# Loading and decoding weight pieces on two separate schedules, and one chunk's P in another place

## The chip, the cores and the metric

The kernel runs on one core of a Trainium2 chip. The metric is the device time of one execution in microseconds (us). The engines are TensorE (PE in the rows, PEld for its weight loads), VectorE (DVE), ScalarE (ACT), GpSimd (POOL) and SyncE (SP, which here only issues transfers).

## The reference

Three parts stand behind one another. The first is a recurrence over 768 steps, for 4 batches and 8 heads, with a state of 40 x 40:

```python
for t in range(S):
    y[:, :, t] = einsum('bhd,bhde->bhe', r_t, state)
    Sa = einsum('bhde,bhe->bhd', state, a_t)
    state = state * w_t[:, :, None, :] - einsum('bhd,bhe->bhde', Sa, b_t)
    state = state + einsum('bhd,bhe->bhde', v_t, k_t)
x = y.transpose(0, 2, 1, 3).reshape(3072, 320)
x = ((x @ w1) * (x @ w2)) @ w3 @ w_out          # w1, w2: 320x1024, w3: 1024x1024, w_out: 1024x320
out = square(maximum(x @ w_in, 0)) @ w_out2     # w_in: 320x2048, w_out2: 2048x320
```

## The kernel before

**The recurrence** runs in 24 chunks of 32 steps. For each chunk the inputs are prepared some chunks ahead: `prep` loads an image of the inputs (`im<-img`, `iw<-img`), forms running products of w with scans on VectorE (`suf`, `wi`) and multiplies them in (`im<-im,wi`, `im<-im,suf`, GpSimd); `pq` makes the chunk's P and Q on TensorE (`Pn`, `qt`, lines 597 to 605); `kb` transposes and stores k and b (`kn`, then `KB_d<-kn`, lines 614 to 619). What is prepared goes through DRAM: `AW_d`, `Q_d` and `KB_d` are written and read again. For four chunks together `solve(k)` (lines 645 to 668) inverts triangular matrices on VectorE: transposes into PT, 31 pairs of a product `tmp` and a subtraction `T`, transposes out to `tt`. The first solve (chunks 0 to 3) is followed by a small `corner` step on TensorE (`x`, `tt`, lines 690 to 701). Each chunk then goes through x0 (`X`), sa (`SA`), sat (`vs`), l (`YI`), z (`YR`) and ys (`RX`, the state for the next chunk, and `yst`, the result, stored as `X_d<-yst`).

**The weights** arrive as 64-bit floats, that is two 32-bit words for each value. A piece (512 KB) is loaded into a `raw` or `early` tile and decoded by four instructions: on ScalarE `wst<-raw` (the high words, line 325) and in place `raw<-raw` (the low words, line 326), on VectorE two that put them together (lines 328 and 330). The 16 pieces of w3 are then folded with w_out on TensorE: 64 products `pw`, `step(f, k)`, four for each piece, into `wph` and `wpl`. The 8 whole pieces and 2 pieces of remaining rows (two loads each) of w1 and w2 are split into a high and a low part: a cast on ScalarE (`w1h<-wst`, line 340), a subtraction on GpSimd (`w1l<-wst,w1h`, line 341). For every two chunks `a_tile` computes 256 columns of (x @ w1) * (x @ w2) and their product with the folded weight (`ab`, line 370; `px`, line 428), as work that fills TensorE between the chunk's steps. When the recurrence is through, the last stage does the third part of the reference (`ph`, line 370; `po`, line 997), which takes the rest of the time.

**What sets the order.** TensorE's order is written by hand: two tables, `OPENING` and `BETWEEN`, say which `prep`, `pq`, `kb`, `corner` and `solve` stand between the steps of the first chunks, and after each step `Fill.pull(gap)` puts in items of a queue (folds, then A tiles). On the other engines a scheduler orders the instructions by priority; the chunk's steps run at a high one, items of the kind "decode" in the queue at none. An item of length 0 is issued when the items ahead of it have been pulled. Each engine does its instructions in its order: one that waits holds what stands behind it. All loads and stores named here are issued by SyncE.

Of the kernel before, what the change touches and what calls it, by code (L numbers as in the profile page):

```python
# [18 lines left out]
DM = 320  # L19
# [29 lines left out]
FOLD_NS = 535  # L49
SPLIT_AT = (8, 13)  # L50
W3_FIRST = 5
FOLD_STAGED = 8
SPLIT_STAGED = 8
# [190 lines left out]
def body(tc, img, rv, rd, vn, vp, raw, w1, w2, w3t, wo, win, wo2, ident, maskt, out, dbg=None):  # L244
# [4 lines left out]
    with (  # L249
# [12 lines left out]
        with right, tc.manual_schedule(engines={mybir.EngineType.PE}):  # L262
# [4 lines left out]
            fill = Fill(tc)  # L267
# [13 lines left out]
            early = True  # L281
# [10 lines left out]
            count = {"fold": 0, "split": 0}  # L292
            bufs = {"raw": WB[0], "wst": WB[1], "split": WB[2]}

            def fetch(pl, K, N, parts, dst=None, tag="fold"):

                place = None
                if early:
                    count[tag] += 1
                    if tag == "split" and count[tag] <= SPLIT_STAGED:  # L300
                        place = staged(ma, ("gh", "gl"), 1024)
                    elif tag == "fold" and not w12 and count[tag] <= FOLD_STAGED:
                        place = staged(wa, ("w1h", "w1l", "w2h"), 640)
                tag = "split" if early and tag == "split" else "wst"
                if dst is not None:
                    o = dst
                else:
                    o = pl.tile([128, K, N], F32, name="wst", tag=tag, bufs=bufs[tag])
                if not is64:
                    for p, f, src in parts:  # L310
                        sp.dma_start(out=o[p, f], in_=src)
                    return o
                if place is not None:
                    rt = place[:, 0:2 * K * N]
                else:
                    rt = pl.tile([128, 2 * K * N], U32, name="raw", tag="raw", bufs=bufs["raw"])
                rv_ = rt.rearrange("p (k n) -> p k n", k=K)
                for p, f, src in parts:
                    sp.dma_start(out=rv_[p, f], in_=src)
                w2_ = rt.rearrange("p (k n j) -> p k n j", k=K, j=2)  # L320
                hi, lo = w2_[:, :, :, 1], w2_[:, :, :, 0]
                ou = o.bitcast(U32)
# [11 lines left out]
            def split_w(pl, src, h, l, j, k):  # L334

                n = 512 if early else 256

                t = fetch(pl, 1, n, [(slice(0, 128), 0, wcols(src, n * j, n)[128 * k:128 * k + 128])], tag="split")
# [4 lines left out]
            def split_r(pl, two):  # L343

                n = 512 if early else 256


                t = fetch(pl, 1, n, [(slice(64 * i, 64 * i + 64), 0, wcols(src, c, n)[256:320])
                                       for i, (src, c, _) in enumerate(two)], tag="split")
                for i, (_, c, r) in enumerate(two):  # L350
                    p, q = slice(64 * i, 64 * i + 64), slice(64 - 64 * i, 128 - 64 * i)
                    f = slice(c, c + n)
                    act.copy(out=r[p, f], in_=t[p, 0])
                    pool.tensor_tensor(out=r[q, f], in0=t[p, 0], in1=r[p, f], op=ALU.subtract)
# [18 lines left out]
            def a_tile(n):  # L373
# [63 lines left out]
                fill.push((0, load, "load"), (0, split, "load"), before="x")  # L437
# [7 lines left out]
            def fold(solved):  # L445
# [9 lines left out]

                def step(f, k):
# [10 lines left out]
                def split12(j):  # L467
# [3 lines left out]
                    for k in range(2):  # L471
                        for src, t in zip((w1, w2), w12):
                            split_w(wf, src, *t[0:2], j, k)
                    split_r(wf, [(src, 512 * j, t[2]) for src, t in zip((w1, w2), w12)])

                hold.append(solved)
                for i in range(8):
                    fetch(wf, 1, DM, [(slice(0, 128), 0, wcols(wo)[128 * i:128 * i + 128, :])], dst=wo_sb[:, i:i + 1])
                for i in range(W3_FIRST):
                    load_w3(i)  # L480
                hold.clear()
                items = []
                for f in range(8):
                    for k in range(8):
                        items.append((FOLD_NS, lambda f=f, k=k: step(f, k), "w"))
                        i = 2 * f + k // 4
                        if k % 4 == 3:
                            if i + W3_FIRST < 16:
                                items.append((0, lambda i=i + W3_FIRST: load_w3(i), "decode"))
                            for j in range(2):  # L490
                                if SPLIT_AT[j] == i:
                                    items.append((0, lambda j=j: split12(j), "decode"))
# [447 lines left out]
            def wu(pl, k):  # L940
                t = fetch(pl, 1, DM, [(slice(0, 128), 0, wcols(wo2)[128 * k:128 * k + 128, :])])
                act.copy(out=wuh[:, k], in_=t[:, 0])
                pool.tensor_tensor(out=wul[:, k], in0=t[:, 0], in1=wuh[:, k], op=ALU.subtract)
# [3 lines left out]
            early = False  # L947
            bufs.update(raw=BB[0], wst=BB[1])
            for j in range(8):
                for k in range(2):  # L950
                    split_w(wst, win, wih, wil, j, k)
                if j < 4:
                    split_r(wst, [(win, 256 * j + 1024 * i, wir) for i in range(2)])
                for k in (2 * j, 2 * j + 1):
                    wu(wst, k)
                if j == 0:
                    b_split(wb, 0, 1)
                fill.pull(BP)
# [178 lines left out]
```

## Time and profile before

| what | us |
| --- | --- |
| median of 3 runs | 1073.65 |
| lowest and highest of them | 1069.87, 1074.45 |
| the profiled execution | 1071.28 |
| its span, from first to last instruction | 1069.5 |
| PE busy | 918.1 (86%) |
| DVE busy | 712.5 (67%) |
| ACT busy | 443.8 (41%) |
| POOL busy | 233.2 (22%) |

All busy times are of the span. They are averages over parts that differ: the recurrence with the A tiles takes until 714 us, the last stage the rest.

### The profile page before, as it was taken

How to read it: one execution, taken by the hardware profiler on the slowest of the kernel's cores; microseconds unless marked ns; L12 is line 12 of the kernel's file. 1: busy time of each engine (PE TensorE's matmuls, PEld its weight loads, DVE VectorE, ACT ScalarE, POOL GpSimd, SP SyncE). 2: the span in 40 equal slices, each digit the busy share in tenths (PEclk: the TensorE clock that was granted, in tenths of full speed). 3: DMA queues.
4: the chain of work that ended last, by engine and by line, in shares of the span. 5: the costliest groups of instructions: out<-in, count | busy, mean ns of one | idle time of the engine just before them, and what ended most of it. 6: DMA issues, size and time to landing. Idle time of an engine off the chain costs nothing.

```text
span 1069.5 us, 29225 instructions
## 1 busy us (share of the span) xinstructions
PE 918.1 (86%) x12240; PEld 822.5 (77%) x12240; DVE 712.5 (67%) x1399; ACT 443.8 (41%) x942; POOL 233.2 (22%) x304
## 2 busy tenths in 40 slices
PE   1327777688989889979899999889999999999997
PEld 1315545588888878979798889868989898898896
DVE  6864879957975997798489444887456554444432
ACT  2424556343434423424343434775334333333332
POOL 0271224433343343533200000652000000000000
PEclk9999888899999999989899999989999999999999
DMA  8976785666666567766644542665122121000001
GB/s 212 307 235 177 209 247 158 171 168 170 163 154 173 148 151 182 170 170 149 164 118 110 136 96 60 171 188 111 30 62 53 59 48 25 2 25 1 18 8 28
DMA packets 208922, 134.45 MB, mean 126 GB/s; under 512 B 143741, under 2 KB 184062, under 8 KB 208368
## 3 DMA queue, kind: packets, MB, share of 16 engines
q1 hardware_dynamic: 201424, 110.61, 40.6%
q0 software_dynamic: 7072, 21.57, 7.1%
q8 instruction: 99, 1.62, 0.7%
q10 hardware_dynamic: 288, 0.33, 0.2%
q14 instruction: 39, 0.32, 0.1%
HBM read 99.27 MB, written 33.19 MB: 124 GB/s over the span
## 4 chain that ended last, share of the span: by engine, by line
PE 48%; DVE 26%; DMA 12%; issue 5%; ACT 4%; POOL 3%; SPq 2%; ACTq 0%; DVEq 0%; POOLq 0%
PE ph L370 16%; PE po L997 15%; PE ab L370 6%; DMA im<-img 5%; DVE tmp L656 4%; PE px L428 4%; DVE T L659 4%; PE pat L800 2%; DVE RX L808 2%; DVE yst L812 2%; DVE gl L408 2%; DVE g L402 1%; DVE wst L328 1%; DVE YI L777 1%; POOL im L584 1%
## 5 line engine op out<-in xcount | busy, mean ns | idle before, releaser
L997 PE MATMUL po<-wul,rh 128*128 128x320 f32 x384 | 118.3, 308 | 0.0
L997 PE MATMUL po<-wuh,rh 128*128 128x320 f32 x384 | 118.0, 308 | 0.0
L997 PE MATMUL po<-wuh,rl 128*128 128x320 f32 x384 | 116.9, 308 | 0.0
L407 ACT CAST gh<-g 128x256 fp32r<-128x256 f32 x96 | 39.0, 406 | 99.8 <-DVE g L402 86.5
L370 PE MATMUL ph<-xh,wih 128*128 128x512 f32 x192 | 76.0, 396 | 0.7 <-issue 0.7
L428 PE MATMUL px<-wph,gh 128*128 128x320 f32 x192 | 68.1, 355 | 9.3 <-DVE x L433 4.8
L370 PE MATMUL ph<-xh,wil 128*128 128x512 f32 x192 | 75.7, 394 | 0.0
L370 PE MATMUL ph<-xl,wih 128*128 128x512 f32 x192 | 75.6, 394 | 0.0
L997 PEld LDWEIGHTS po<-wul,rh 128*128 128x128 f32 x384 | 72.0, 188 | 4.2
L997 PEld LDWEIGHTS po<-wuh,rh 128*128 128x128 f32 x384 | 72.0, 188 | 3.8
L997 PEld LDWEIGHTS po<-wuh,rl 128*128 128x128 f32 x384 | 71.6, 188 | 0.6 <-DVE rl L984 0.6
L800 PE MATMUL pat<-YI,YR 128*40 128x72 f32 (+1 forms) x1536 | 58.8, 240 | 13.7 <-DVE qt L602 8.1
L800 PEld LDWEIGHTS pat<-YI,YR 128*40 128x40 f32 x1536 | 54.5, 127 | 19.2 <-DVE qt L602 9.7
L408 DVE TENSOR_TENSOR gl<-g,gh 128x256 fp32r<-128x256 f32 x96 | 48.2, 503 | 30.0 <-ACT gh L407 29.6
L401 ACT COPY a_sb<-ab 128x256 f32<-128x256 f32 x96 | 35.6, 371 | 76.4 <-PE ab L370 75.9
L656 DVE TENSOR_TENSOR tmp<-PT,T 128x31 f32<-128x31 f32 (+20 forms) x170 | 64.9, 382 | 3.4
L659 DVE TENSOR_TENSOR T<-T,tmp 128x31 f32<-128x31 f32 (+20 forms) x170 | 64.5, 380 | 3.0
L428 PE MATMUL px<-wph,gl 128*128 128x320 f32 x192 | 63.2, 329 | 3.4 <-DVE gl L408 3.4
L584 POOL TENSOR_TENSOR im<-im,suf 104x256 f32<-104x256 f32 x80 | 64.4, 836 | 0.0
L428 PE MATMUL px<-wpl,gh 128*128 128x320 f32 x192 | 62.4, 325 | 0.0
L370 PE MATMUL ph<-xq,wir 128*128 128x512 f32 x192 | 60.1, 394 | 0.0
L370 PE MATMUL ab<-xh,w1h 128*128 128x256 f32 x192 | 57.9, 302 | 2.5 <-ACT xh L357 2.2
(539 smaller groups left out, 2444.3 us busy)
## 6 DMA issues: line engine op xcount, KB each, us to landing
raw<-w3t SPq DMA_DIRECT2D x16, 512.0 KB
YR<-KB_d SPq DMA_DIRECT2D x48, 160.0 KB
im<-img POOLq DMA_DIRECT2D x28, 240.0 KB, 4.5
wt<-AW_d SPq DMA_DIRECT2D x24, 214.5 KB
raw<-wo SPq DMA_DIRECT2D x16, 320.0 KB
RX<-vp SPq DMA_DIRECT2D x24, 208.0 KB
vs<-rv SPq DMA_DIRECT2D x24, 208.0 KB
KB_d<-kn POOLq DMA_DIRECT2D x14, 320.0 KB, 5.3
```

Source lines behind the costliest of these rows:

```text
L370: mm(out=ps, lhsT=seq[i][0], rhs=seq[i][1], start=(i == 0), stop=(i == 7))
L401: act.copy(out=a_sb, in_=ps[:, 0])
L407: act.copy(out=t["gh"][:, ff], in_=g)
L408: dve.tensor_tensor(out=t["gl"][:, ff], in0=g, in1=t["gh"][:, ff], op=ALU.subtract)
L428: mm(out=ps, lhsT=a_, rhs=b_, start=(k == 0 and i == 0), stop=(k == 7 and i == 2))
L584: eng.tensor_tensor(out=kb[:, g, :, :, j], in0=kb[:, g, :, :, j], in1=sg, op=ALU.mult)
L656: dve.tensor_tensor(out=tv, in0=Pv[:, :, s, s + 1:n].unsqueeze(3).to_broadcast(sh), in1=Tv[:, :, s, 0:s + 1].unsqueeze(2).to_broadcast(sh) ...
L659: return dve.tensor_tensor(out=o, in0=o, in1=tv, op=ALU.subtract).ins
L800: mm(out=ps[64 * y:64 * y + D, b, 72 * z:72 * z + n], lhsT=YR[:, u], rhs=YI[:, u, 0:n], start=True, stop=True, tile_position=(0, 64 * y))
L808: dve.tensor_tensor(out=o, in0=v[r, :, :, C:72], in1=decay.unsqueeze(3).to_broadcast([D, 2, HZ, D]), op=ALU.mult)
L812: dve.tensor_tensor(out=yst[r, :, 2 * g:2 * g + 2].rearrange("p z b t -> p b z t"), in0=v[r, :, :, 0:C], in1=wt[c][r, 2 * g:2 * g + 2, :, ...
L997: mm(out=po[j][g], lhsT=a_, rhs=b_, start=(ff == 0 and i == 0), stop=(ff == 15 and i == 2))
```

## The change

A function `fetch` that loaded and decoded a piece becomes two, `fetch` (load) and `decode`. The pieces of w3 are now put in the queue apart: behind the four folds of piece i stands the decode of piece i + 3 (`AHEAD`) and the load of piece i + 6; before, the load and decode of piece i + 5 stood there. The pieces of w1 and w2 stood in two blocks of 5, behind w3 pieces 8 and 13 (`SPLIT_AT`); now there is one piece at a time, `load12(m)` behind w3 piece m + 3 and `decode12(m)` two pieces later, all of them loaded into the staging tiles `gh` and `gl`, where before the first 8 were. Folds of the last quarter of w3 get the kind "last", and the load and split of A tile 0 are put ahead of those, with kind "decode". The P and Q of chunk 5 (`("pq", 5)`) move from ahead of chunk 0's sa to behind its ys. The weights of the last stage are loaded by the new functions in the same order. The line numbers of the changed file differ: ScalarE's decode is in lines 312 and 313, the weight loads in line 299.

```diff
 BETWEEN = {
     (0, "start"): (("prep", 5), ("prep", 6)),
-    (0, "x0"): (("corner", 0), ("pq", 5)),
+    (0, "x0"): (("corner", 0),),
...
-    (0, "ys"): (("kb", 5), ("pq", 6), ("kb", 6)),
+    (0, "ys"): (("pq", 5), ("kb", 5), ("pq", 6), ("kb", 6)),
...
-SPLIT_AT = (8, 13)
-W3_FIRST = 5
-FOLD_STAGED = 8
-SPLIT_STAGED = 8
+AHEAD = 3
+SPLIT_FROM = 3
...
+            def decode(pl, raw_, dst=None, tag="wst"):
+
+                rt, K, N = raw_
+                o = pl.tile([128, K, N], F32, name="wst", tag=tag, bufs=bufs[tag]) if dst is None else dst
+                ou = o.bitcast(U32)
...
+            def piece_w(src, h, l, n, j, k):
+
                 f = slice(n * j, n * j + n)
-                act.copy(out=h[:, k, f], in_=t[:, 0])
-                pool.tensor_tensor(out=l[:, k, f], in0=t[:, 0], in1=h[:, k, f], op=ALU.subtract)
...
+                def load(pl, place=None):
+                    return fetch(pl, 1, n, [(slice(0, 128), 0, wcols(src, n * j, n)[128 * k:128 * k + 128])], place)
+
+                def split(t):
+                    act.copy(out=h[:, k, f], in_=t[:, 0])
+                    pool.tensor_tensor(out=l[:, k, f], in0=t[:, 0], in1=h[:, k, f], op=ALU.subtract)
+
+                return load, split
...
-                fill.push((0, load, "load"), (0, split, "load"), before="x")
+                fill.push((0, load, "load" if n else "decode"), (0, split, "load" if n else "decode"),
+                          before="x" if n else "last")
...
-                for i in range(W3_FIRST):
-                    load_w3(i)
+                for i in range(3):
+                    load_w3(i)
+                for i in range(8):
+                    decode(wf, wos[i], wo_sb[:, i:i + 1])
+                for i in range(AHEAD):
+                    decode_w3(i)
+                    load_w3(i + 3)
                 hold.clear()
                 items = []
-                for f in range(8):
-                    for k in range(8):
-                        items.append((FOLD_NS, lambda f=f, k=k: step(f, k), "w"))
-                        i = 2 * f + k // 4
-                        if k % 4 == 3:
-                            if i + W3_FIRST < 16:
-                                items.append((0, lambda i=i + W3_FIRST: load_w3(i), "decode"))
-                            for j in range(2):
-                                if SPLIT_AT[j] == i:
-                                    items.append((0, lambda j=j: split12(j), "decode"))
+                then = lambda fn, i: items.append((0, lambda: fn(i), "decode"))
+                for i in range(16):
+                    f = i // 2
+                    for k in range(4 * (i % 2), 4 * (i % 2) + 4):
+                        items.append((FOLD_NS, lambda f=f, k=k: step(f, k), "last" if f > 5 else "w"))
+                    if i + AHEAD < 16:
+                        then(decode_w3, i + AHEAD)
+                    if i + AHEAD + 3 < 16:
+                        then(load_w3, i + AHEAD + 3)
+                    m = i - SPLIT_FROM
+                    if 0 <= m - 2 < 10:
+                        then(decode12, m - 2)
+                    if 0 <= m < 10:
+                        then(load12, m)
```

On ScalarE, chunk 0, from the corner's first `tt` to its second; before:

```order
L701 COPY tt<-pat 16x8x16 x4
L325 ACTIVATE wst<-raw 128x512
L326 ACTIVATE raw<-raw 128x512 x3
L601 COPY Pn<-pat 128x2x4x32
L326 ACTIVATE raw<-raw 128x512
L754 COPY SA<-pat 128x8x40
L764 COPY YI<-SA 32x8x40 x4
L761 COPY vs<-pat 104x4x4x32
L697 ACTIVATE x_837<-pat 128x128
L701 COPY tt<-pat 16x8x16 x4
```

and in the changed kernel (lines 713, 766, 776, 773 and 709 are tt, SA, YI, vs and x):

```order
L713 COPY tt<-pat 16x8x16 x4
L766 COPY SA<-pat 128x8x40
L312 ACTIVATE wst<-raw 128x512
L313 ACTIVATE raw<-raw 128x512
L776 COPY YI<-SA 32x8x40 x4
L773 COPY vs<-pat 104x4x4x32
L313 ACTIVATE raw<-raw 128x512 x2
L709 ACTIVATE x_791<-pat 128x128
L313 ACTIVATE raw<-raw 128x512
L713 COPY tt<-pat 16x8x16 x4
```

The copy SA moved from behind five decode instructions to ahead of them, YI and vs from behind five to behind two, and Pn, which belongs to the P of chunk 5, left this place.

On ScalarE, from chunk 1's copies kn (the second is of `kb` 6) to its vs; before:

```order
L618 COPY kn<-pat 128x8x40 x2
L601 COPY Pn<-pat 128x2x4x32
L618 COPY kn<-pat 128x8x40 x2
L744 ACTIVATE X_101<-pat 128x320
L325 ACTIVATE wst<-raw 128x512
L325 ACTIVATE wst<-early 128x512
L326 ACTIVATE early<-early 128x512
L754 COPY SA<-pat 128x8x40
L764 COPY YI<-SA 32x8x40 x4
L761 COPY vs<-pat 104x4x4x32
```

and in the changed kernel, from the decode behind the second Pn on (lines 630, 756 and 329 are kn, X and the cast):

```order
L313 ACTIVATE early<-early 128x512
L630 COPY kn<-pat 128x8x40 x2
L329 CAST w1h<-wst 128x512
L329 CAST w2h<-wst 128x512
L312 ACTIVATE wst<-early 128x512
L756 ACTIVATE X_101<-pat 128x320
L313 ACTIVATE early<-early 128x512
L329 CAST w1h<-wst 128x512
L312 ACTIVATE wst<-raw 128x512
L766 COPY SA<-pat 128x8x40
L776 COPY YI<-SA 32x8x40 x4
L312 ACTIVATE wst<-early 128x512
```

Ahead of this kn the changed kernel has four decode instructions of the first w1 and w2 pieces, and behind it come two casts and a high half ahead of X; ahead of vs, which is some rows further down, two more low halves follow, of a split piece and of a w3 piece.

On SyncE, around the store of `kb` 5 at the end of chunk 0; before:

```order
L815 DMA X_d<-yst 40x4x128
L619 DMA KB_d<-kn 128x640
L815 DMA X_d<-yst 40x4x128
L319 DMA early<-w 128x1024
L541 DMA im<-img 40x1536 x2
L605 DMA Q_d<-qt 128x256
```

and in the changed kernel:

```order
L827 DMA X_d<-yst 40x4x128 x2
L299 DMA early<-w 128x1024 x2
L631 DMA KB_d<-kn 128x640
L617 DMA Q_d<-qt 128x256
L553 DMA im<-img 40x1536 x2
L631 DMA KB_d<-kn 128x640
```

Two loads of split pieces moved to ahead of the store KB_d; before, one stood behind it.

## Rows read from the trace of the kernel before

**Rows 1.** Busy time by stretch: PE, PEld, DVE, ACT, POOL, clock, DMA share.

```profile
130.00:214.00 84.00, 60.09 (x900) 44.66 (x900) 75.38 (x149) 41.68 (x86) 33.21 (x34) 0.85 0.69 195
214.00:714.00 500.00, 453.38 (x7888) 420.12 (x7888) 369.91 (x822) 212.36 (x507) 152.23 (x220) 0.95 0.59 149
714.00:1069.00 355.00, 348.37 (x1920) 312.91 (x1920) 177.26 (x257) 138.62 (x241) 9.97 (x11) 1.00 0.18 40
```

**Rows 2.** ACT in order of time, chunk 0: start, length, [idle before].

```profile
62.72 1.07 ACT L701 COPY tt<-pat 16x128 f32<-16x128 f32 x4 [0.83 <-PE pat L693]
74.66 0.66 ACT L325 ACTIVATE wst<-raw 128x512 f32<-128x512 f32 x1 [10.87 <-DMA raw<-w3t]
...
82.22 0.67 ACT L326 ACTIVATE raw<-raw 128x512 uint32<-128x512 uint32 x1 [1.61 <-DMA raw<-w3t]
82.80 0.40 ACT L754 COPY SA<-pat 128x320 f32<-128x320 f32 x1
...
85.12 0.59 ACT L761 COPY vs<-pat 104x512 f32<-104x512 f32 x1
```

**Rows 3.** SP's issues of transfers in order of time, chunks 0 and 1.

```profile
70.37 1.50 SPq L319 DMA_DIRECT2D raw<-w3t  x3
71.95 0.43 SPq L585 DMA_DIRECT2D AW_d<-wi  x1
...
97.13 0.36 SPq L619 DMA_DIRECT2D KB_d<-kn  x1
...
106.52 0.35 SPq L319 DMA_DIRECT2D early<-w  x1
```

**Rows 4.** DVE in order of time, chunk 0.

```profile
80.12 1.26 DVE L566 TENSOR_TENSOR_SCAN wi<-iw,inv 104x528 f32<-104x528 f32 x1 [2.80 <-DMA AW_d<-wi]
...
85.85 1.26 DVE L566 TENSOR_TENSOR_SCAN wi<-iw,inv 104x528 f32<-104x528 f32 x1
87.78 1.39 DVE L777 TENSOR_TENSOR YI<-pat,msk 64x512 f32<-64x512 f32 x2 [0.67 <-PE pat L772]
91.45 0.99 DVE L808 TENSOR_TENSOR RX<-pat,gc 40x320 f32<-40x320 f32 x2 [2.29 <-PE pat L800]
```

**Rows 5.** ACT in order of time, chunk 1.

```profile
101.54 0.76 ACT L618 COPY kn<-pat 128x320 f32<-128x320 f32 x2 [4.29 <-DMA KB_d<-kn]
102.18 0.46 ACT L744 ACTIVATE X<-pat 128x320 f32<-128x320 f32 x1
...
106.70 0.59 ACT L761 COPY vs<-pat 104x512 f32<-104x512 f32 x1
...
111.57 0.67 ACT L325 ACTIVATE wst<-early 128x512 f32<-128x512 f32 x1 [2.72 <-DMA early<-w]
...
112.69 0.26 ACT L697 ACTIVATE x<-pat 128x128 f32<-128x128 f32 x1
```

**Rows 6.** PE in order of time, chunks 0 and 1.

```profile
72.59 1.18 PE L597 MATMUL pat<-im 40*32 40x64 f32 x64 [9.93 <-POOL im L578]
...
116.06 1.58 PE L785 MATMUL pat<-idt,RX 40*104 40x40 f32 x16 [2.38 <-DVE YI L777]
...
121.07 2.66 PE L800 MATMUL pat<-YI,YR 128*40 128x72 f32 x64
```

**Rows 7.** POOL in order of time, chunk 1.

```profile
106.66 1.18 POOL L578 TENSOR_TENSOR im<-im,wi 104x512 f32<-104x512 f32 x1 [8.05 <-DMA im<-img]
...
110.84 1.26 POOL L341 TENSOR_TENSOR w1l<-wst,w1h 128x512 fp32r<-128x512 f32 x1
```

**Rows 8.** DVE in order of time, the solve of chunks 4 to 7.

```profile
129.86 2.08 DVE L649 STREAM_TRANSPOSE PT<-Pn 128x256 f32<-128x256 f32 x4
...
137.09 0.69 DVE L328 SCALAR_TENSOR_TENSOR wst<-wst,raw 128x512 uint32<-128x512 uint32 x1 [2.10 <-DMA im<-img]
...
140.03 0.81 DVE L358 TENSOR_TENSOR xl<-xf,xh 128x512 fp32r<-128x512 f32 x1 [1.42 <-ACT xh L357]
...
213.77 0.60 DVE L662 STREAM_TRANSPOSE tt<-T 128x256 f32<-128x256 f32 x1
```

More of the change, by code (lines that the diff above doesn't have):

```diff
@@ L280, in body @@
             staging = {}
-            early = True
             ma = right.enter_context(tc.tile_pool(name="ma", bufs=1, side="right"))
@@ L291, in body, with fetch @@
             hold = []
-            count = {"fold": 0, "split": 0}
             bufs = {"raw": WB[0], "wst": WB[1], "split": WB[2]}
[L295 to L306, printed above, removed]
-                else:
[L308 to L316, printed above, removed]
+            def fetch(pl, K, N, parts, place=None):
+                if place is not None:
+                    rt = place[:, 0:sc * K * N]
+                else:
+                    rt = pl.tile([128, sc * K * N], U32, name="raw", tag="raw", bufs=bufs["raw"])
                 rv_ = rt.rearrange("p (k n) -> p k n", k=K)
                 for p, f, src in parts:
-                    sp.dma_start(out=rv_[p, f], in_=src)
+                    sp.dma_start(out=rv_[p, f], in_=src.bitcast(U32))
+                return rt, K, N
+            def decode(pl, raw_, dst=None, tag="wst"):
+                rt, K, N = raw_
+                o = pl.tile([128, K, N], F32, name="wst", tag=tag, bufs=bufs[tag]) if dst is None else dst
+                ou = o.bitcast(U32)
+                if not is64:
+                    act.copy(out=o, in_=rt.bitcast(F32).rearrange("p (k n) -> p k n", k=K))
+                    return o
                 w2_ = rt.rearrange("p (k n j) -> p k n j", k=K, j=2)
                 hi, lo = w2_[:, :, :, 1], w2_[:, :, :, 0]
-                ou = o.bitcast(U32)
                 act.activation(out=o, in_=hi.bitcast(F32), func=AF.Copy, scale=2.0 ** -112)
@@ L454, in load_w3, with decode_w3 @@
                         512 * g:512 * g + 512, :].rearrange("(k p) f -> p k f", p=128))])
+                def decode_w3(i):
+                    w3[i] = decode(wf, w3[i])
                 def step(f, k):
@@ L470, in split12 @@
                             wa.tile([128, FA], F32R, name=f"w{i}r"),) for i in "12"])
[L471 to L474, printed above, removed]
+                        for j in range(2):
+                            for k in range(2):
+                                w12s.extend(piece_w(src, *t[0:2], 512, j, k) for src, t in zip((w1, w2), w12))
+                            w12s.append(piece_r([(src, 512 * j, t[2]) for src, t in zip((w1, w2), w12)], 512))
@@ L476, in fold, with decode12 @@
+                    loaded[m] = w12s[m][0](wf, staged(ma, ("gh", "gl"), 1024))
+                def decode12(m):
+                    w12s[m][1](decode(wf, loaded.pop(m), tag="split"))
                 hold.append(solved)
+                wos = [fetch(wf, 1, DM, [(slice(0, 128), 0, wcols(wo)[128 * i:128 * i + 128, :])],
+                             staged(wa, ("w1h", "w1l", "w2h"), 640)) for i in range(8)]
+                for i in range(3):
+                    load_w3(i)
                 for i in range(8):
-                    fetch(wf, 1, DM, [(slice(0, 128), 0, wcols(wo)[128 * i:128 * i + 128, :])], dst=wo_sb[:, i:i + 1])
@@ L938, in b_split, with piece_u, load, split @@
                 xt[j] = (xh, xl, xq)
[L940 to L943, printed above, removed]
+            def piece_u(k):
+                def load(pl):
+                    return fetch(pl, 1, DM, [(slice(0, 128), 0, wcols(wo2)[128 * k:128 * k + 128, :])])
+                def split(t):
+                    act.copy(out=wuh[:, k], in_=t[:, 0])
+                    pool.tensor_tensor(out=wul[:, k], in0=t[:, 0], in1=wuh[:, k], op=ALU.subtract)
+                return load, split
             b_load(wb, 0, 1)
             wst = tc.alloc_tile_pool(name="wst", bufs=1, side="left")
-            early = False
             bufs.update(raw=BB[0], wst=BB[1])
             for j in range(8):
-                for k in range(2):
-                    split_w(wst, win, wih, wil, j, k)
+                todo = [piece_w(win, wih, wil, 256, j, k) for k in range(2)]
                 if j < 4:
-                    split_r(wst, [(win, 256 * j + 1024 * i, wir) for i in range(2)])
-                for k in (2 * j, 2 * j + 1):
-                    wu(wst, k)
+                    todo.append(piece_r([(win, 256 * j + 1024 * i, wir) for i in range(2)], 256))
+                todo += [piece_u(k) for k in (2 * j, 2 * j + 1)]
+                for load, split in todo:
+                    split(decode(wst, load(wst)))
                 if j == 0:
```

26 lines of the change are left out of this document (13 added, 13 removed).

## The prediction

> **What bounds the kernel now.** First the windows by stage [rows 1]: from 214 us on the program is bound by TensorE (453.38 of 500 us busy, then 348.37 of 355), and before that, from 130 to 214 us, by VectorE (75.38 of 84 us, TensorE 60.09). The order of TensorE's work is the same in both kernels but for the matrix products of chunk 5's P, and what is late or early at 214 us moves everything behind it. So the question is when the VectorE-bound solve of chunks 4 to 7 begins (its first transposes, PT, stand at 129.86) and when it ends (tt at 213.77) [rows 8]. It begins when chunk 1 is through, so I read the engines' timelines over chunks 0 and 1, about 59 to 130 us, to see what each small step waits for.
>
> Chunk 0 is held by the decode of w3. ScalarE has one queue: behind tt at 62.72 stands the first decode instruction of a w3 piece, which begins at 74.66 after 10.87 us of waiting for its transfer; three more low halves wait in turn, the last at 82.22, and only then come the copies SA (82.80) and vs (85.12) [rows 2]. The pieces were issued at 70.37 [rows 3]. TensorE was held as well: P of chunk 5 stood ahead of sa and waited 9.93 us for GpSimd, to 72.59 [rows 6]. The chunk's last VectorE step, RX, starts at 91.45 [rows 4].
>
> Chunk 1 ends with ys at 121.07 [rows 6]. Here the copy kn waited 4.29 us for a store to DRAM (KB_d) to land, X followed at 102.18, vs at 106.70, and the corner's x at 112.69 behind a w1 piece that was waited for (2.72 us) [rows 5].
>
> **The change, part by part.**
>
> *Chunk 0 (P of chunk 5 moved, first decode order).* With P gone from ahead of sa, sa needs only tt (62.72 + 1.07 us, [rows 2]), so the SA copy, which now stands right behind tt on ScalarE, runs at about 65 instead of 82.80. That itself gives nothing: the YI copies and vs now stand behind one w3 piece (two instructions) instead of four. The piece arrives as before, 74.66; two instructions of 0.66 us bring the queue to 76.0, and vs, which came 2.32 us after the beginning of SA (82.80 to 85.12, the YI copies in between, [rows 2]), to 78.3 instead of 85.12. VectorE's YI followed vs by 2.66 us (85.12 to 87.78, [rows 2, 4]), which gives 81.0, but it stands behind the scan wi, 80.12 to 81.38, so 81.4 instead of 87.78; RX would be ready 3.67 us later (91.45 - 87.78), 85.1, but stands behind the next wi, 85.85 + 1.26, so 87.1 [rows 4]. **Chunk 0 ends 4.35 us earlier** (91.45 - 87.1). The cover that ends the gain is the two scans, which wait for transfers that the change doesn't move.
>
> *Chunk 1 (P of chunk 5 moved here, w1 and w2 one piece at a time).* Behind ys(0) TensorE now does P of chunk 5, then kb 5. The store KB_d of kb 5 would be issued at 97.13 - 4.35 + 1.18 (the length of those products, [rows 6]) = 94.0. Before, one w1 piece was issued behind it; now two 512 KB pieces, w1 and w2, are issued just ahead of it on the same queue [rows 3]. On ScalarE, kn of kb 6 now stands behind the decode of those two pieces and waits for the store as well. Two bounds for the landing: with nothing ahead the store of 97.13 let kn go at 101.54, 4.41 us [rows 3, 5]; the store AW_d<-wi, issued at 71.95 right behind three 512 KB pieces, let its reader go at 80.12, 8.17 us [rows 3, 4]. So 98.4 to 102.2; I take a value near the second, since the case is like it but for two pieces in place of three: kn stands at 101.5, as before, and **the 4.35 us are gone**.
>
> The page "DMA: Bandwidth & Descriptors" of the Trainium skill (section "Queues, rings and completion order") says that on each DMA engine descriptors are consumed in the order of the ring. By it the store can't pass the two pieces, and kn is at the late bound; without it, at 98.4, and the fast rival below has more of a chance. The 8.17 us behind three pieces against 4.41 behind none agree with the rule.
>
> From kn the queue of ScalarE is longer than before. Two casts, taken as long as a decode instruction of the same tile (0.67 us, 111.57 in [rows 5]), then the high half of a third piece, which needs a buffer that GpSimd's subtraction frees (1.26 us, [rows 7]): kn ends at 102.3, the first cast at 103.0, its subtraction at 104.2, the high half at 104.9: X at about 105.1 instead of 102.18 (at best 102.9, if the buffer is free). Then, ahead of vs, now stand a low half of a split piece and a low half of a w3 piece. That w3 piece is issued behind the store AW_d<-im, which waits for GpSimd's im (106.66 after 8.05 us, [rows 7]) and for what GpSimd now does ahead of it, two subtractions, of which I count one: 109.7. A 512 KB piece took 5.05 us from issue to reader (106.52 to 111.57, [rows 3, 5]): the low half at 114.8, **vs at 115.5 instead of 106.70** (at best 112.2, if im is not later and the piece goes ahead of it). The corner's x stands behind two more low halves, at about 120 instead of 112.69; from x to ys were 8.4 us, of which TensorE's z waited 2.38 for VectorE's YI [rows 6], which is done by then: ys(1) at about 126.1 instead of 121.07 (at best 122). The solve then begins 8.79 us behind ys (129.86 - 121.07), less two decode instructions that now stand elsewhere (about 1 us): 133.9. Together **+4.0 us at the beginning of the solve; bounds +0.3 (both best cases) and +4.2**.
>
> *The solve.* The order of VectorE's work from the solve's first transposes to its last holds the same kinds and number of instructions but two less. Of the 84 us it is idle for under 9 [rows 1], and I see two waits that the new order may fill: 2.10 us for a transfer ahead of a decode (137.09) and 1.42 us for ScalarE's xh (140.03) [rows 8]. The second goes, since A tile 0's split now stands lower and something that is ready goes first; of the first I count nothing, because a start that is 4 us later brings the transfers for later steps no nearer. **-1.5 us**; bounds: -7 (nearly all idle time goes) and +4 (two more waits of 2.1 us, as rival 2).
>
> *Decode "three ahead".* On VectorE as many decode instructions (16) stand ahead of the solve's transposes as before, so this moves nothing out of the VectorE-bound stretch: 0. It costs what it adds in waits, which is in the terms above. If that count were lower, each would be worth about 0.69 us (137.09's length, [rows 8]) and nothing more.
>
> *214 us to the end.* TensorE's rows are the same and SyncE's nearly so; TensorE is busy for 91% and 98% [rows 1], so a shift at 214 is carried to the end: 0 more. The rewritten loads of the last stage keep their order: 0, at most 1 us.
>
> **Sum:** +4.0 - 1.5 = +2.5 us. The profiled execution took 1071.28 us (span 1069.5), so 1073.8; the median of the runs is 2.4 above that execution, so for the median **1076**. About 0.5% (5.4 us, bounds 1068.3 and 1079.0) is what a measurement of this kernel can tell from no change.
>
> **The rivals.**
>
> *1, faster.* The 4.35 us of chunk 0 survive. That needs the two pieces to land before the store of kb 5 matters (kn by 98.4) and the w3 piece ahead of vs to land without waiting for im. Then the solve also begins early enough to be fed and 2.10 + 1.42 us of its waits go: 1073.65 - 4.35 - 3.52 = 1065.8. For it: the DMA engines are not full (0.69 busy from 130 to 214 us, [rows 1]), and SA is free early. Against it: the waits for large transfers in [rows 2, 5], which show that ScalarE's queue passes on each landing.
>
> *2, slower.* The low halves ahead of vs recur in chunk 2, inside the solve: a wait of ScalarE for a w3 piece, as at 82.22 [rows 2], holds SA or vs, and VectorE, which has no other work ready, idles. Two more waits of the size of 2.10 us: 4.0 + 4.2 = +8.2, 1081.9. It decides if vs of chunk 2 comes more than the start's 4 us later. Against it: VectorE has decode work of its own there to fill in.
>
> *3, it doesn't do what it says.* The decodes are no further ahead at the solve (16 and 16), chunk 0's gain and chunk 1's loss cancel: 1073.65, within 0.5%.
>
> **How the numbers follow.** The forecast (+2.5, its own range 1070 to 1079) has 0.38, rival 3 0.15, both within 0.5%: same 0.53. Rival 1 has 0.20 (faster), rival 2 0.27 (slower). The range reaches to both rivals and the bounds about them, 1064 to 1084.
>
> **What would show it.** SA of chunk 0 at about 65 and RX at about 87 (step 1); kn of kb 6 behind a landing, near 101.5, X near 105 (step 2); vs of chunk 1 waiting for raw<-w3t near 115 (step 3); PT near 134; tt of the solve near 216; and from there the same length to the end. The prediction is wrong if vs of chunk 1 is below 110, PT below 130, or the solve's length from PT to tt differs by over 4 us from 83.9.

## The result, and the profile after

| | median, us | lowest to highest | profiled execution, us (span) |
| --- | --- | --- | --- |
| before (8 runs) | 1074.1 | 1069.87 to 1077.85 | 1071.28 (1069.5) |
| changed (8 runs) | 1085.61 | 1079.32 to 1091.9 | 1085.53 (1083.7) |

The ratio is 1.0114, with a 95% interval of 1.0087 to 1.0142: slower by 1.1%, where 1076 us (no change that can be told) was forecast, and above the range of 1064 to 1084 us. The medians differ by 11.5 us, the two profiled executions by 14.2; what is read from a profile below belongs to one execution. Medians here and below leave out two slow executions, one of e10 (1089.28 us) and one of e11 (1542.78 us).

ScalarE over chunks 0 and 1 of the changed kernel, in order of time (start, length, engine, line, operation, idle time before it and what ended it); the rows answer to [rows 2, 5]:

```profile
70.11 0.43 ACT L766 COPY SA<-pat 128x320 f32<-128x320 f32 x1 [4.61 <-PE pat L764]
...
75.97 0.66 ACT L312 ACTIVATE wst<-raw 128x512 f32<-128x512 f32 x1 [5.43 <-DMA raw<-w3t]
...
79.07 0.59 ACT L773 COPY vs<-pat 104x512 f32<-104x512 f32 x1
...
101.04 0.66 ACT L312 ACTIVATE wst<-early 128x512 f32<-128x512 f32 x1 [6.08 <-DMA early<-w]
...
103.92 0.73 ACT L630 COPY kn<-pat 128x320 f32<-128x320 f32 x2
...
107.54 0.67 ACT L312 ACTIVATE wst<-early 128x512 f32<-128x512 f32 x1 [1.22 <-POOL w1l L330]
...
108.11 0.42 ACT L756 ACTIVATE X<-pat 128x320 f32<-128x320 f32 x1
...
111.81 0.66 ACT L313 ACTIVATE early<-early 128x512 uint32<-128x512 uint32 x1 [3.28 <-DMA early<-w]
...
112.88 0.65 ACT L312 ACTIVATE wst<-raw 128x512 f32<-128x512 f32 x1
...
120.39 0.65 ACT L313 ACTIVATE raw<-raw 128x512 uint32<-128x512 uint32 x1 [3.40 <-DMA raw<-w3t]
...
120.95 0.57 ACT L773 COPY vs<-pat 104x512 f32<-104x512 f32 x1
...
125.06 0.26 ACT L709 ACTIVATE x<-pat 128x128 f32<-128x128 f32 x1
```

SA and vs of chunk 0 are earlier, as forecast (79.07 against 85.12). In chunk 1 every step that was named is there, each later than I worked out (a high half is the decode instruction for a piece's high words, a low half the one for its low words): kn behind the decode of the first two split pieces (103.92), X behind a high half that waited 1.22 us for GpSimd's subtraction (108.11 against 102.18), a low half that waited 3.28 us for its transfer, then vs behind a low half of w3 that waited 3.40 us (120.95 against 106.70), then x (125.06 against 112.69).

SyncE's issues answer to [rows 3]: two loads ahead of the store, and the w3 piece of the low half at 120.39, issued only at 116.69.

```profile
94.70 0.85 SPq L299 DMA_DIRECT2D early<-w  x2
...
95.64 0.37 SPq L631 DMA_DIRECT2D KB_d<-kn  x1
...
116.69 0.40 SPq L299 DMA_DIRECT2D raw<-w3t  x1
```

VectorE answers to [rows 4, 8]. RX of chunk 0 comes 3.7 us earlier, PT 9.0 later, tt 10.6 later; at 146.59 VectorE waits inside the solve, for ScalarE's high half, which stood behind a low half that waited 5.05 us for its w3 piece:

```profile
86.45 1.26 DVE L578 TENSOR_TENSOR_SCAN wi<-iw,inv 104x528 f32<-104x528 f32 x1
87.74 0.99 DVE L820 TENSOR_TENSOR RX<-pat,gc 40x320 f32<-40x320 f32 x2
...
115.96 0.66 DVE L317 SCALAR_TENSOR_TENSOR wst<-raw,wst 128x512 uint32<-128x512 uint32 x1
...
138.82 2.12 DVE L661 STREAM_TRANSPOSE PT<-Pn 128x256 f32<-128x256 f32 x4
...
146.59 0.69 DVE L315 SCALAR_TENSOR_TENSOR wst<-wst,raw 128x512 uint32<-128x512 uint32 x1 [2.96 <-ACT wst L312]
...
224.36 0.60 DVE L674 STREAM_TRANSPOSE tt<-T 128x256 f32<-128x256 f32 x1
```

TensorE answers to [rows 6], and shows the beginning of the last stage:

```profile
104.71 1.29 PE L754 MATMUL pat<-RX,XL 128*32 128x40 f32 x64 [9.29 <-ACT kn L630]
...
131.71 2.19 PE L812 MATMUL pat<-YI,YR 128*40 128x72 f32 x62 [0.39 <-ACT YR L800]
...
725.80 0.47 PE L363 MATMUL ph<-xh,wih 128*128 128x512 f32 x1 [2.81 <-POOL wil L330]
```

The first ph of the last stage begins at 725.80, after a wait of 2.81 us for GpSimd. In the kernel before, that place reads as follows (a row that was not shown above):

```profile
714.08 0.47 PE L370 MATMUL ph<-xh,wih 128*128 128x512 f32 x1 [0.66 <-issue]
```

So the last stage begins 11.72 us later. From there to the end of the span it takes 1083.7 - 725.80 = 357.90 us, against 1069.5 - 714.08 = 355.42. The difference of the spans, 14.2 us, is made up so: 8.96 at PT (138.82 - 129.86), 1.63 in the solve (85.54 against 83.91), -1.02 over the A tiles (from tt to the end of the work ahead of ph's wait), 2.15 in the wait for ph (2.81 against 0.66), 2.48 in the last stage.

In the last stage ScalarE's first relu (`r_`), which stands 2.09 us behind the first ph in the kernel before, stands 6.10 us behind it in the changed kernel, since decodes of the last weights come ahead of it there:

```profile
716.17 0.60 ACT L981 ACTIVATE r__10604<-ph 128x512 f32<-128x512 f32 x1
```

```profile
731.13 0.49 ACT L313 ACTIVATE raw<-raw 128x320 uint32<-128x320 uint32 x1 [2.85 <-DMA raw<-wo]
...
731.90 0.58 ACT L998 ACTIVATE r__10603<-ph 128x512 f32<-128x512 f32 x1
```

### The profile page after: what moved, and what is told of

Its sections match the earlier page's. It is cut to its first block, busy times and chain, and to the rows that moved or that the text cites. A ratio compares the mean times of both kernels' runs of the same rounds, so it can differ in the third digit from the quotient of the medians.

```text
span 1083.7 us, 29228 instructions
## 1 busy us (share of the span) xinstructions
PE 920.0 (85%) x12240; PEld 821.9 (76%) x12240; DVE 715.9 (66%) x1399; ACT 441.7 (41%) x942; POOL 231.1 (21%) x304
## 4 chain that ended last, share of the span: by engine, by line
PE 44%; DVE 25%; DMA 16%; ACT 6%; issue 4%; POOL 2%; SPq 2%; ACTq 0%; DVEq 0%; POOLq 0%
PE ph L363 16%; PE po L1014 15%; PE ab L363 5%; DVE tmp L668 4%; DMA im<-img 4%; DVE T L671 4%; DVE RX L820 3%; DVE yst L824 3%; PE px L421 2%; DMA raw<-w3t 2%; DMA X_d<-yst 2%; PE pat L812 2%; DVE gl L401 2%; DVE wst L315 2%; DMA xr<-X_d 2%
## 5 line engine op out<-in xcount | busy, mean ns | idle before, releaser
L400 ACT CAST gh<-g 128x256 fp32r<-128x256 f32 x96 | 38.9, 405 | 97.8 <-DVE g L395 85.5
L668 DVE TENSOR_TENSOR tmp<-PT,T 128x31 f32<-128x31 f32 (+20 forms) x170 | 67.4, 397 | 3.4
```

What stands on the lines that cost most here:

```text
L400: act.copy(out=t["gh"][:, ff], in_=g)
L668: dve.tensor_tensor(out=tv, in0=Pv[:, :, s, s + 1:n].unsqueeze(3).to_broadcast(sh), in1=Tv[:, :, s, 0:s + 1].unsqueeze(2).to_broadcast(sh) ...
```

## The experiments

Theory A, formed on these rows: ScalarE does its queue in order, and a copy of the recurrence that stands behind a decode pays for that decode's transfer. Its rivals are named in the expectations. The table has the medians, the ratio to the kernel before with its interval, and from each profiled execution the start of PT, the length of the solve (from PT to its last tt) and the last stage from the first ph to the end of the span. One profile doesn't give PT to the microsecond: up to PT e6 and e11 have the order of before on ScalarE, VectorE, GpSimd and SyncE, e5 that of e2 and e10 that of the changed kernel, and their PTs differ from those by 0.2 to 2.7 us. The profiled execution of e6 (1060.27 us) was the fastest of its 12.

| run | median | ratio, 95% interval | PT | solve | last stage |
| --- | --- | --- | --- | --- | --- |
| before | 1074.1 | | 129.86 | 83.9 | 355.4 |
| changed | 1085.61 | 1.0114 (1.0087, 1.0142) | 138.82 | 85.5 | 357.9 |
| e1 | 1080.56 | 1.0071 (1.0045, 1.0096) | 139.36 | 84.4 | 356.8 |
| e2 | 1078.53 | 1.0065 (1.0040, 1.0090) | 131.24 | 83.8 | 358.0 |
| e3 | 1075.53 | 1.0034 (1.0011, 1.0057) | 133.91 | 86.4 | 355.8 |
| e4 | 1075.42 | 1.0031 (1.0006, 1.0056) | 129.03 | 88.8 | 356.8 |
| e5 | 1066.55 | 0.9935 (0.9908, 0.9962) | 128.58 | 82.3 | 355.7 |
| e6 | 1066.22 | 0.9950 (0.9923, 0.9977) | 131.27 | 79.4 | 355.7 |
| e7 | 1075.43 | 1.0011 (0.9987, 1.0035) | 133.28 | 84.1 | 357.0 |
| e8 | 1074.82 | 1.0040 (1.0008, 1.0071) | 134.05 | 79.4 | 358.0 |
| e9 | 1073.30 | 0.9994 (0.9966, 1.0022) | 134.41 | 81.9 | 356.9 |
| e10 | 1079.18 | 1.0053 (1.0023, 1.0083) | 140.35 | 80.9 | 356.5 |
| e11 | 1066.81 | 0.9957 (0.9932, 0.9983) | 129.69 | 83.2 | 357.5 |
| e12 | 1074.02 | 1.0011 (0.9988, 1.0035) | 132.74 | 84.1 | 356.8 |
| e13 | 1075.41 | 1.0018 (0.9987, 1.0049) | 131.87 | 83.3 | 358.0 |
| e14 | 1080.51 | 1.0067 (1.0044, 1.0090) | 129.57 | 89.0 | 357.2 |

The runs of before beside e1 to e14 had medians of 1071.83 to 1073.22 us.

### The two halves of the change: e1 and e2

```diff
# e1, on the kernel before
-    (0, "x0"): (("corner", 0), ("pq", 5)),
+    (0, "x0"): (("corner", 0),),
-    (0, "ys"): (("kb", 5), ("pq", 6), ("kb", 6)),
+    (0, "ys"): (("pq", 5), ("kb", 5), ("pq", 6), ("kb", 6)),
# e2: the changed kernel with these two lines put back
```

> The kernel before, with nothing but the P of chunk 5 moved behind chunk 0's ys. Theory A (the move alone puts ScalarE's queue of chunks 0 and 1 in another order, and the waits for transfers in that queue cost the time): about as slow as the changed kernel, +9 to +13 us over before, vs of chunk 1 near 120, PT near 138. Theory B (the new schedule of loads and decodes of the weights costs it): within 3 us of before, PT near 130. Theory C (most of it comes from the last stage): +3 to +5 us.

> The changed kernel with the P of chunk 5 back ahead of chunk 0's sa, so that only the weights' schedule is new. Theory A: within 3 us of before, vs of chunk 1 near 107, PT near 130. Theory B: +9 to +13 us, like the changed kernel. Theory C: +3 to +5 us if the last stage's order comes with the weights' part.

Both halves cost time, 8.6 and 6.6 us against the median of the runs of before beside them (1071.97), and neither theory had it whole. In e1 chunk 1 reads as in the changed kernel:

```profile
109.11 0.42 ACT L744 ACTIVATE X<-pat 128x320 f32<-128x320 f32 x1
...
121.58 0.57 ACT L761 COPY vs<-pat 104x512 f32<-104x512 f32 x1
```

PT stands at 139.36: all of chunk 1's loss comes with the P that was moved, though the weights' code is the old one. The scheduler's order of instructions on ScalarE in chunks 0 and 1 is that of the changed kernel, and so is that on VectorE, GpSimd and SyncE. In e2 chunk 1 is as in before (vs at 109.10, PT at 131.24), and the time is lost in two other places. At the vs of chunk 4 two low halves of the last stage's weights wait ahead of it:

```profile
217.59 1.86 ACT L776 COPY YI<-SA 32x320 f32<-32x320 f32 x4
...
221.99 0.44 ACT L313 ACTIVATE raw<-raw 128x256 uint32<-128x256 uint32 x1 [2.55 <-DMA raw<-win]
...
224.34 0.43 ACT L313 ACTIVATE raw<-raw 128x256 uint32<-128x256 uint32 x1 [1.91 <-DMA raw<-win]
...
225.31 0.57 ACT L773 COPY vs<-pat 104x512 f32<-104x512 f32 x1
```

Before, that vs stood at 221.24. TensorE waits there twice, for tt and for vs:

```profile
215.78 1.29 PE L764 MATMUL pat<-X,tt 32*32 32x40 f32 x64 [4.66 <-DVE tt L674]
...
225.94 1.97 PE L784 MATMUL pat<-RT,vs 104*64 104x64 f32 x32 [3.09 <-ACT vs L773]
```

and in the 20 us behind it has the granted clock of the lower level for a good part of the time (the columns are busy time and instructions of PE, PEld, DVE, ACT, POOL, then clock, DMA share and GB/s). For before and for e2:

```profile
220.00:240.00 20.00, 17.32 (x327) 15.98 (x325) 10.60 (x22) 7.94 (x20) 6.74 (x10) 1.00 0.62 155
```

```profile
220.00:240.00 20.00, 16.91 (x220) 15.96 (x221) 5.13 (x11) 6.92 (x17) 2.91 (x5) 0.78 0.39 102
```

220 matmuls took 16.91 us where 327 took 17.32. X of chunk 5 is at 246.84, 7.0 us later than before (239.84); by the end of the A tiles 4.7 us are left of it, 1.3 of which were there at tt already. The other place is the last stage: ph waits 2.07 us and the stage lasts 358.0 us. The first of the two places is e2's own. In the changed kernel the vs of chunk 4 stands ahead of those two low halves (230.53 against 233.66 and 235.41), and X of chunk 5, 8.6 us later than before, is no later than PT had made it.

### Decodes kept from ahead of a copy: e3 to e8

The rule is an order on ScalarE alone; at_ is 1 in e3 and e4, for decodes whose program text stands between the vs of chunk 1 and that of chunk 3, 6 in e5 and e6 for those of the last stage, both in e7 and e8, from which the edit is shown. The work stays the same.

```diff
+                at_ = 6 if NCH - 1 in vs_in else 1 if 3 not in vs_in else None
+                with tc.issue_after(vs_in[at_]) if at_ in vs_in else nullcontext():
-                act.activation(out=o, in_=hi.bitcast(F32), func=AF.Copy, scale=2.0 ** -112)
-                act.activation(out=lo, in_=lo, func=AF.Copy, scale=2.0 ** -29, bias=LOW)
+                    act.activation(out=o, in_=hi.bitcast(F32), func=AF.Copy, scale=2.0 ** -112)
+                    act.activation(out=lo, in_=lo, func=AF.Copy, scale=2.0 ** -29, bias=LOW)
...
+                    vs_in[c] = act.copy(out=vs_t[c][0:104, :, C:64] ...).ins
```

> The changed kernel, but ScalarE's decode instructions that belong to program text behind chunk 1's vs may not be issued ahead of that vs. Theory A: chunk 1 loses its waits for w1, w2 and w3 pieces: X of chunk 1 near 104 instead of 108.1, vs near 109 instead of 120.95, PT near 130; some decode work moves into the VectorE-bound solve (at most 8 instructions of 0.69 us); 1073 to 1080 us. Theory B or C: chunk 1 is not where the time goes, 1083 to 1088 us as the changed kernel.

> The kernel before with the same rule (decodes of later program text not ahead of chunk 1's vs). Theory A: there only three decode instructions stood ahead of vs and none waited long: vs of chunk 1 1 to 2 us earlier than 106.7, the time within 3 us of before. If holding decodes back has a price of its own (decode late in the solve, folds late on TensorE), it shows here as +2 us or more without any gain to set against it.

e3 took 10 us off the changed kernel's median (1085.61 to 1075.53); vs of chunk 1 stands at 111.97 and PT at 133.91, less than expected. Of the 11.8 us between the two profiles 4.9 are at PT; 4.2 are the wait for ph and the last stage, which is back at 355.8 although the rule doesn't name its weights. e4 shows the price: in the kernel before the same rule lengthens the solve from 83.9 to 88.8 us, with 39 of VectorE's decode instructions in it instead of 36, since decodes that are kept back come into the stretch that VectorE bounds. It gains nothing against that (vs of chunk 1 at 107.19).

> The kernel of e2 (new weights' schedule, P of chunk 5 in its old place), but ScalarE's decodes of the last stage's weights, which stood ahead of the vs of chunk 4, may not be issued ahead of the vs of chunk 6. Theory A (ScalarE's queue: a copy of the recurrence behind a decode that waits for its transfer): e2 lost its time there, X of chunk 5 comes some 5 to 7 us earlier than in e2 (246.84), and the last stage's r_ stands as in before; 1069 to 1074 us. Rival D (the loss of e2 is folds and A tiles that come at other times on TensorE, and the clock it is granted): X of chunk 5 within 2 us of e2's, 1077 to 1080 us.

> The kernel before with that same rule for the last stage's weights alone. Theory A: before too waits for these pieces ahead of X, SA and vs of chunk 4 (0.4 to 2.1 us at a time, 6 us in all), so it becomes 1 to 4 us faster than before. Rival D: within 1 us of before.

Here theory A holds and D falls: e5 is 12 us below e2, with X of chunk 5 at 236.72 (e2: 246.84), and the last stage is back at 355.7. Both gains are larger than theory A's ranges (e5 below 1069, e6 over 4 us faster). In e6 nothing waits for these weights ahead of vs of chunk 4, where before waited 2.14 and 1.75 us. Before, then e6:

```profile
215.54 0.45 ACT L326 ACTIVATE raw<-raw 128x256 uint32<-128x256 uint32 x1 [2.14 <-DMA raw<-win]
...
220.90 0.43 ACT L326 ACTIVATE raw<-raw 128x256 uint32<-128x256 uint32 x1 [1.75 <-DMA raw<-win]
```

```profile
208.26 0.43 ACT L746 ACTIVATE X<-pat 128x320 f32<-128x320 f32 x1
...
212.26 0.43 ACT L756 COPY SA<-pat 128x320 f32<-128x320 f32 x1 [0.32 <-PE pat L754]
...
216.30 0.59 ACT L763 COPY vs<-pat 104x512 f32<-104x512 f32 x1
```

e6 and e5 are faster than both kernels. The rule did a second thing, which the expectations don't name: eight of VectorE's decode instructions for these weights (3.8 us in before) stand inside the VectorE-bound solve in before and in e2, and none in e5 and e6. The solve is 1.5 us shorter in e5 than in e2, and 4.5 in e6 than in before; the stretch from the last tt to the end of the A tiles, where the copies no longer wait, is 9.1 and 8.2 us shorter. No run parts the two. In e6 one of the decodes that are kept back waits for its piece at 276.92, for 0.69 us.

> The changed kernel with the rule of e3 (decodes not ahead of vs of chunk 1) and that of e5 (the last stage's not ahead of vs of chunk 6). Theory A: e3's gain and e5's add up, 1068 to 1073 us. Rival D: as e3, 1074 to 1077 us.

> The kernel of e1 (only the P of chunk 5 moved) with both rules. Theory A: like e7, 1067 to 1073 us; where e7 and e8 differ by more than 3 us, the weights' schedule costs or gives something apart from ScalarE's order around vs. Rival D: 1074 us or more.

These missed theory A's ranges and lie in rival D's: with the P moved, both rules give 1075, not 1070. PT is still 3 to 4 us late, and the last stage is long again. e8 shows the first as a wait of kn for a store, 7.9 us behind its issue (94.22) and behind two loads of 512 KB:

```profile
93.24 0.88 SPq L319 DMA_DIRECT2D early<-w  x2
...
94.22 0.37 SPq L621 DMA_DIRECT2D KB_d<-kn  x1
```

```profile
102.11 0.75 ACT L620 COPY kn<-pat 128x320 f32<-128x320 f32 x2 [8.39 <-DMA KB_d<-kn]
```

### The store behind the loads, and what is next: e9, e12, e10

```diff
# e9 on e7, e12 on e8
-                for p, f, src in parts:
-                    sp.dma_start(out=rv_[p, f], in_=src.bitcast(U32))
+                with tc.issue_after(kb_in[6]) if 6 in kb_in and 3 not in vs_in else nullcontext():
+                    for p, f, src in parts:
+                        sp.dma_start(out=rv_[p, f], in_=src.bitcast(U32))
# e10: the changed kernel with the rule of e5 alone
```

> The kernel of e7 (changed kernel, decodes not ahead of vs of chunk 1 nor, for the last stage's weights, of chunk 6), and weight loads of later program text are not issued ahead of the store KB_d of kb 6. In the kernel of e8 the copy kn waited 8.39 us for the store of kb 5, which stood behind two 512 KB loads. Theory A (the store waits behind the loads): the wait falls to 4.5 us or less, X of chunk 1 near 101 instead of 105.3, PT near 130 instead of 133.3; 1069 to 1072 us against e7's 1075.4. Rival E (the store takes as long without them, or the time at PT is not carried to the end): PT within 1 us of e7, 1074 to 1077 us.

> The kernel of e8 (P of chunk 5 moved, both rules) with the loads rule of e9 as well. Theory A: chunk 0 keeps its gain of 4 us and chunk 1 has no wait for weights left, PT near 129 to 130; 1068 to 1072 us, 3 to 6 us below e8 (1074.8). Rival E: as e8.

The store was as theory A says: without the loads ahead of it kn goes 3.57 us behind its issue (97.14), and X (101.76) and vs are within 0.5 us of before. In e12, which differs from e8 by this rule alone, it goes 3.61 us behind (94.35 to 97.96):

```profile
97.14 0.37 SPq L634 DMA_DIRECT2D KB_d<-kn  x1
```

```profile
100.71 0.75 ACT L633 COPY kn<-pat 128x320 f32<-128x320 f32 x2 [3.58 <-DMA KB_d<-kn]
...
107.09 0.59 ACT L776 COPY vs<-pat 104x512 f32<-104x512 f32 x1
...
118.43 0.28 ACT L712 ACTIVATE x<-pat 128x128 f32<-128x128 f32 x1
```

But PT didn't move in e9 (134.41), and in e12 by 1.3 us (132.74). In e9 the decodes now stand ahead of the corner's x, which comes at 118.43, and TensorE waits 7.14 us for it:

```profile
118.76 0.72 PE L708 MATMUL pat<-x,early 32*16 32x16 f32 x64 [7.14 <-ACT x L712]
```

The time that theory A expected (1069 to 1072 and 1068 to 1072 us) was missed; e12 is as rival E has it, e9 0.7 us below E's range.

> The changed kernel with the rule for the last stage's weights alone (not ahead of vs of chunk 6); chunk 1 is left as in the changed kernel, and the last stage's r_ stands as in before. If the parts add up as e2 against e5 says (that rule gave 12 us there), PT is still near 139 and the time 1073 to 1078 us, 8 to 12 us below the changed kernel. If the chunk 1 loss is nearly all of the changed kernel's loss, 1082 us or more.

It took 6.4 us off the changed kernel's median. In the profiles 4.5 us lie between the two: 3.5 less in the last stage (wait 0.7, then 356.5 us), 4.7 less in the solve, which the eight VectorE instructions have left, and 3.7 more elsewhere; chunk 1 keeps its loss (PT at 140.35). The median lies above the 1073 to 1078 that the sum of e1, e2 and e5 gave, so the parts don't simply add up: the two waits ahead of vs of chunk 4, which e5 took away from e2, weren't there in the changed kernel.

### The last stage: e11

```diff
# on e6; lo_in: the low-half instructions in program order
-                act.activation(out=r_, in_=ps, func=AF.Relu)
+                with tc.issue_after(lo_in[34 + 31]) if j == 0 and ff == 0 else nullcontext():
+                    act.activation(out=r_, in_=ps, func=AF.Relu)
```

> The kernel of e6, with the first r_ of the last stage held behind one decode instruction of its weights that stood three places further down on ScalarE, so that r_ stands where the changed kernel has it. If the order of r_ and decodes sets the last stage's length: from the first ph to the end 357 to 358 us instead of 355.7, and 1 to 3 us more than e6 (1066.2). If not: within 0.5 us of 355.7.

The first r_, the relu of the first ph, comes at 712.31 behind a decode that waited 1.23 us for its piece:

```profile
710.84 0.50 ACT L328 ACTIVATE raw<-raw 128x320 uint32<-128x320 uint32 x1 [1.23 <-DMA raw<-wo]
...
712.31 0.60 ACT L984 ACTIVATE r__10604<-ph 128x512 f32<-128x512 f32 x1
```

and the last stage takes 357.5 us instead of 355.7, with r_ 6.2 us behind the first ph (2.1 in e6). TensorE's `po` then waits 1.0 us for VectorE's `rl` in all, 1.7 in the changed kernel and 0.2 in e6. The size is that of the profile; in the medians 0.6 us can't be told from nothing.

### The corner: e13 and e14

```diff
-                with tc.issue_after(vs_in[at_]) if at_ in vs_in else nullcontext():
+                with tc.issue_after(yr_in[1] if at_ == 1 and 1 in yr_in else vs_in[at_]) if at_ in vs_in else nullcontext():
```

> The kernel of e9, with the decodes of later program text kept behind chunk 1's YR instead of its vs, so that the corner's x has at most one of them ahead. Theory A (each copy of the recurrence on ScalarE pays for the decode ahead of it): x of the corner near 112 instead of 118.4, PT near 128 instead of 134.4; 1067 to 1071 us if the solve then is no longer than in e9, more if the decodes are missed there. Rival F (the moved P itself costs it, by the work it adds behind chunk 0's ys): PT 132 or later, 1073 us or more.

> The kernel of e13 with the P of chunk 5 in its old place, ahead of chunk 0's sa. Theory A: chunk 0 is 2 to 4 us longer, no wait for decodes in chunk 1 in either; within 4 us of e13. Rival F: 5 us or more faster than e13, like e5 and e6 (1066.4).

In e13 PT comes 2.5 us earlier than in e9 (131.87), not 6, and the time is in F's range, above theory A's 1067 to 1071. The corner's x comes at 107.91, 4.8 us earlier than in before, and TensorE's z hardly earlier (115.64 against 116.06): VectorE's YI, for which it waits, stands behind two scans, the first of which waited 10.44 us for GpSimd's im, and two decode instructions (1.3 us). So no transfer of a weight piece bounds chunk 1 up to there any more. F falls by e14: with the P in its old place it is 5 us slower than e13, not faster; that is also more than theory A allowed. Its solve lasts 89.0 us. VectorE in e13 and in e14, PT and last tt:

```profile
131.87 2.12 DVE L664 STREAM_TRANSPOSE PT<-Pn 128x256 f32<-128x256 f32 x4
...
215.19 0.61 DVE L677 STREAM_TRANSPOSE tt<-T 128x256 f32<-128x256 f32 x1
```

```profile
129.57 2.07 DVE L664 STREAM_TRANSPOSE PT<-Pn 128x256 f32<-128x256 f32 x4
...
218.54 0.61 DVE L677 STREAM_TRANSPOSE tt<-T 128x256 f32<-128x256 f32 x1
```

Decodes taken from ahead of one copy stand ahead of the next, or in the solve: 34 of VectorE's decode instructions stand there in e13 and e14, 28 in e5, e6 and e9.

## Why the prediction was wrong

**Chunk 0: right.** SA at 70.11 (65 forecast; TensorE's sa began at 64.72, but its last 16 products at 69.57), vs at 79.07 (78.3), RX at 87.74 (87.1): 3.7 us earlier, 4.35 forecast. RX stands right behind the scan wi (86.45), the cover that was named.

**Chunk 1: the mechanism was right, the size wrong.** The term "+4.0 us at the beginning of the solve; bounds +0.3 and +4.2" measured +8.96, over twice the value and outside its bounds, of which the upper one was no bound: it lies 0.2 above the value, where kn's late bound alone (102.2) lies 0.7 above the 101.5 that was taken. kn came at 103.92 instead of 101.5: not the store alone but the pieces themselves, which landed 6.3 us (94.70 to 101.04) and more after their issue, with four decode instructions ahead of kn. X came at 108.11, not 105.1, vs at 120.95, not 115.5, x at 125.06, not 120, ys at 131.0 to 131.7, not 126.1. The step that failed is the issue of the w3 piece ahead of vs: I took it as set by the store AW_d<-im ahead of it on SyncE, at 109.7. That store was issued at 110.51, but the piece at 116.69, because SyncE waited 5.4 us in between for VectorE's second decode instruction on an earlier w3 piece, which reads the `raw` buffer that the load fills; it starts at 115.96 and ends 0.07 us before the issue. The high half of a w3 piece stands at 112.88, behind the split piece that waited until 111.81. So one late landing on ScalarE put off a decode, the decode a buffer, the buffer a load, and the load vs; the wait is read from the trace, and no run gave the load another buffer.

**The weights' part: wrong.** "Decode 'three ahead'" was put at 0 from the order in which VectorE does its decodes up to the solve, and "214 us to the end" at 0 more from the rows of TensorE and SyncE; ScalarE's order behind the solve stands in neither. e2 shows 0.65% for it, at places that I had taken as unchanged: the vs of chunk 4 (4.1 us later), the clock behind it, and the last stage (ph's wait and 2.5 us), which the prediction bounded by 1 us. In the changed kernel the part behind the solve measured 3.6 us: 4.6 in the wait for ph and the last stage, less 1.0 over the A tiles.

**The solve: wrong.** -1.5 forecast, +1.6 measured. VectorE is idle for 8.9 us of it, 8.6 before, and busy for 1.4 us more (76.69 against 75.29) with one instruction less. The two waits that were named [rows 8] went, the xh wait as forecast; in their place VectorE waited three times for a high half on ScalarE, 6.7 us in all, of which 2.96 us at 146.59.

**The rivals.** Rival 2 had the direction and the kind of event (a low half ahead of SA or vs), but put it in chunk 2 and on top of +4.0; it came in chunk 1, and in e2 in chunk 4. vs of chunk 2 is 9.6 us later, little more than PT. Rival 3's count of 16 decodes was true and decided nothing. The way it came out, slower, had 0.27.

**What was the cause, then.** Shown: the P's place alone gives chunk 1's loss (e1), 9.0 of the 14.2 us between the profiles; the weights' part alone costs 0.65% (e2), at the vs of chunk 4, a wait that the changed kernel doesn't have, and in the last stage, a loss that it has; of the last stage's 2.5 us, the place of r_ gives about 1.8, by one profile (e11). An order rule on ScalarE takes 10 us off the changed kernel (e3, of which 4.9 at PT) and 12 off e2 (e5, part of it by VectorE's work leaving the solve). Not shown: what else of chunk 1's loss the decodes cost, since each rule moves them elsewhere. Open: with all rules the moved P still stands at 1073 to 1075, 7 to 9 us above e5. Of that, 1 to 2 us are the last stage's length, 1 to 2.5 the wait for ph, 3 to 6 PT, and 1 to 4 lie from the last tt to the end of the A tiles; why, is not settled. It need not be the P: e14, which has these rules and the P in its old place, stands 14 us above e5, so the rules on chunk 1 cost time of their own.

## What to carry to other kernels

Where a scheduler sets an engine's order, moving one step on TensorE can move work of quite another kind on ScalarE; compare the whole order, on every engine and to the end, and read for each copy of the critical loop what stands ahead of it and what that waits for. A decode that waits for its transfer is free only behind the copies of the loop: here an order of a few instructions (e6, 0.5%) gave a gain where the schedule of loads gave a loss, in part because it also took work out of the stretch that VectorE bounds. Keeping work back has a price too, in the next stretch that another engine bounds (e4, e14), so look for one where the work finds nothing to hold up.

## What the runs showed of the hardware

A store issued right behind two 512 KB loads let its reader go 7.9 us after its issue (e8), without them 3.6 us (e12, and e9). This agrees with the page "DMA: Bandwidth & Descriptors" of the Trainium skill, section "Queues, rings and completion order", by which a DMA engine takes descriptors in the order of its ring. The rows don't tell that apart from transfers that share the bandwidth.

Behind waits TensorE had the lower clock for some microseconds. In e2 the granted clock was 0.50 (the level of 1.2 GHz, of 2.4) from 216 to 222 us, behind the wait of 4.66 us, and again from 226 to 232, behind that of 3.09; the mean from 220 to 240 us was 0.78. In the kernel before it was 0.50 from 208 to 216, behind waits of 1.90 and 2.23 us with 0.27 us of work between them, and stayed at 1.00 from 218 on, through a wait of 1.72 us ahead of vs (221.85).
